# Cached attention decode: longer rows a load, another order of keys, scores after PV

## The chip, the cores and the metric

The kernel runs on one core of one Trainium2 chip. The metric is the time of one execution on the device in microseconds; lower is better. Runs of the kernel before took 1207.76 to 1209.6 us, with a median of 1208.69.

## What is computed

One decode step of a network with two kinds of layers, twice over the same weights and caches: attention over a long cache, then a small SiLU block.

```python
B, Sq, D = 8, 1, 512
Hq, Hkv, Sk, Dh = 32, 8, 8192, 128

def _A_ref(x, k_cache, v_cache, wq, wo):
    q = (x @ wq).reshape(B, Sq, Hq, Dh)              # to (B, Hq, Sq, Dh)
    k = jnp.repeat(k_cache, rep, axis=1)             # rep = 4 query heads a cache head
    v = jnp.repeat(v_cache, rep, axis=1)
    scores = jnp.einsum("bhqd,bhkd->bhqk", q, k) * (Dh ** -0.5)
    p = _softmax(scores, axis=-1)
    o = jnp.einsum("bhqk,bhkd->bhqd", p, v)
    return o.reshape(B, Sq, Hq * Dh) @ wo

def _B_ref(x, w1, w2):                               # F = 1792
    return _silu(x @ w1) @ w2

x = x + _A_ref(_layernorm(x), K, V, wq, wo)
x = x + _B_ref(_layernorm(x), w1, w2)
x = x + _A_ref(_layernorm(x), K, V, wq, wo)
x = x + _B_ref(_layernorm(x), w1, w2)
```

All arrays are bf16. Each of the two caches has 8 batches x 8 heads x 8192 keys x 128 numbers, 134 MB, and both attention layers read both of them.

## The kernel before

**Tasks.** A task is one (layer, batch, cache head). There are 128 of them, and `make_tasks` (L141) lays them out in one list in which the two layers are mixed: while layer 0 works on batch b + 1, layer 1 works on batch b. A task has 8 steps ("positions"; `GPT = 8`), a step covers 8 chunks of 128 keys, and two steps make a granule of 2048 keys, which is the unit of a load: 512 KB, 128 partitions with 4096 bytes each. A head has 4 granules of K and 4 of V.

**Kept heads.** The last 18 granules of K of a batch (half of head 3, heads 4 to 7) stay in SBUF in their transposed form from layer 0 until layer 1 has used them; the layer-1 tasks of these heads ("kept tasks") load only V and transpose nothing. All other tasks are "streaming tasks". For each batch the list has a run of five layer-1 tasks with kept K, then the five layer-0 tasks that fill these heads for the next batch, then five or six streaming tasks.

**Slots and the planner.** SBUF has an arena of 27 slots of one granule. `plan_loads` (L172) lists all 880 loads. Each has a step at which it is needed (`need`) and one after which its slot is free again (`free`). The list is sorted by need, each load takes the slot that comes free first, and `after` is the step after which SP may issue it. `issue` (L352) sends it from SP's queue; SP waits there until the last readers of the slot are done, and everything behind it waits too.

**The main loop** (L748) goes over the steps p and emits, in this order, for all engines:

- `emit_t_until(p + LT)` with `LT = 2`: K of step p + 2 is transposed on TensorE (L433, 8 transposes into one of 3 PSUM banks) and copied back into its own slot by VectorE (L441) or ScalarE (L439, 3 of 8);
- at odd p, first the scores of the granule of steps p - 1 and p (`emit_s`, L464: 4 matmuls of 512 columns), then PV for the two steps 13 and 12 back (`emit_pv`, L537: 2 x 8 matmuls);
- a part of the softmax of the task before: row maximum (L475) and `spread` (L477) at phase 0; a matmul with `ones` that hands every partition the maxima (L485), then `own`, `shift` and the exponential (L488 to L495) at phase 1; the sums (L501, L504) at phase 3; the transposes of P and the copy into `PT` (L513, L517) at phase 4, one step before the first PV that reads it;
- one piece of the "chain", where one is in progress: once layer 0's attention of batch b is complete, the rest of that batch's way to layer 1's query (wo, layer norm at L559 to L602, w1, SiLU, w2, layer norm, wq; matmuls at L613 and L631) is done in small pieces, one or two a step, and has to be through before the first layer-1 task of that batch;
- the normalisation of a finished task (L551) and `issue_until(p)`, which emits the loads whose `after` has come.

Each load has a semaphore of its slot, so the engines wait for a slot's own load. TensorE, VectorE, ScalarE and SP each work in program order. At the end come the sums of heads for layer 1, the last SiLU block for all batches, and the store.

Of the kernel before, what the change touches and what calls it, by code (L numbers as in the profile page):

```python
# [5 lines left out]
HQ = 32  # L6
# [7 lines left out]
GPT = 8  # L14
GPG = 2
NSLOT = 27
KEEP = 18
LT = 2
PRE = 10
LP = 12  # L20
# [4 lines left out]
NPT = 2  # L25
NQB = 2
NST = 4
# [102 lines left out]
class Load:  # L130


    __slots__ = ("kind", "b", "g", "k", "need", "free", "slot", "after")

    def __init__(self, kind, b, g, k, need, free):
        self.kind, self.b, self.g, self.k = kind, b, g, k
        self.need, self.free = need, free
        self.slot, self.after = None, None
# [32 lines left out]

def plan_loads(tasks, kept, nslot, ngran):  # L172

    at = {t: i for i, t in enumerate(tasks)}
    loads = []
    for i, (layer, b, g) in enumerate(tasks):
        for k in range(ngran):
            i0 = i * GPT + k * GPG
            if layer == 0 or (g, k) not in kept:
                need = -1 if i0 < PRE else i0 - LT  # L180
                last = i if layer or (g, k) not in kept else at[(1, b, g)]
                loads.append(Load("K", b, g, k, need, last * GPT + (k + 1) * GPG - 1))
            loads.append(Load("V", b, g, k, i0 + GPG - 1 + LP, i0 + GPG - 1 + LP))
    loads.sort(key=lambda d: (d.need, d.kind))
    free = [(-2, s) for s in range(nslot)]
    for d in loads:
        free.sort()
        d.after, d.slot = free.pop(0)
        assert d.after < d.need or d.need == -1 and d.after == -2, (d.kind, d.need, d.after)
        free.append((d.free, d.slot))  # L190
    return loads
# [18 lines left out]
def _build(ctx, nc, A_x, A_k_cache, A_v_cache, A_wq, A_wo, B_w1, B_w2, out):  # L210
# [59 lines left out]
    QB = [sb([128, NGRAN - 1 + QUAD], BF16, "QB") for _ in range(NQB)]  # L270
    at1 = [sb([128, HQ], BF16, "at1") for _ in range(3)]
    at2 = sb([128, HQ, B], BF16, "at2")
    vr = sb([128, B], FP32, "vr")
    yr = sb([128, B], FP32, "yr")
    tr = sb([128, B], FP32, "tr")
    s1 = sb([128, B], FP32, "s1")
    s1a = sb([128, B], FP32, "s1a")
    xc = sb([128, KT, B], FP32, "xc")
    sq = sb([128, KT, B], FP32, "sq")
    xnT = sb([128, KT, B], BF16, "xnT")  # L280
    eh = sb([128, FT * B], FP32, "eh")
    hsT = sb([128, FT * B], BF16, "hsT")
# [3 lines left out]
    PT = [sb([128, CPB, NQ * USED], BF16, "PT") for _ in range(NPT)]  # L286
    ones = sb([128, 128], FP32, "ones")
    hm = sb([128, REP], FP32, "hm")
    real = sb([128, 1], FP32, "real")
    far = sb([128, NQ * USED], FP32, "far")  # L290
    rowmax = sb([128, 1], FP32, "rowmax")
    spread = sb([128, NQ * USED], FP32, "spread")
    own = sb([128, NQ * USED], FP32, "own")
    shift = sb([128, 1], FP32, "shift")
    rs = [sb([128, 1], FP32, "rs") for _ in range(NST)]
    ssm = [sb([128, REP], FP32, "ssm") for _ in range(NST)]
    ssa = [sb([128, REP], FP32, "ssa") for _ in range(NST)]
    rcp = [sb([128, REP], FP32, "rcp") for _ in range(NST)]

# [52 lines left out]
    def issue(d):  # L352
        cache = A_k_cache if d.kind == "K" else A_v_cache
        src = cache[d.b, d.g].rearrange("(k p c) d -> k p (c d)", k=NGRAN, p=128)[d.k]
        dst = ARENA[:, d.slot * SLOT:(d.slot + 1) * SLOT]
        dma(sp, dst, src, slsem[d.slot], writes=[r_half(d.slot, 0), r_half(d.slot, 1)])
        (k_slot if d.kind == "K" else v_slot)[(d.b, d.g, d.k)] = d.slot

    with nc.Block() as block:

        @block.sync
        def _(sync_eng):
# [11 lines left out]
            op(dve, lambda: dve.memset(ones[:, :], 1.0), writes=["ones"])  # L374
            for n in range(NQB):
                op(pool, lambda n=n: pool.memset(QB[n][:, :], 0.0), writes=[f"QB{n}"])
# [4 lines left out]
                    hm[:, :], lanes.rearrange("p c (r k) -> p r c k", k=NGRAN), AX.XY, ALU.add),  # L381
                reads=["ident"], writes=["hm"],
            )
            op(dve, lambda: dve.tensor_reduce(real[:, :], hm[:, :], AX.X, ALU.add), reads=["hm"], writes=["real"])
            for c in range(NQ):
                op(dve, lambda c=c: dve.tensor_scalar(
                    far[:, c * USED:(c + 1) * USED].rearrange("p (r k) -> p r k", k=NGRAN),
                    hm[:, :].unsqueeze(2).to_broadcast([128, REP, NGRAN]), real[:, 0:1], -FAR,
                    op0=ALU.subtract, op1=ALU.mult),
                   reads=["hm", "real"], writes=["far"])  # L390
# [15 lines left out]
            for _n in range(NGRAN):  # L406
                issue(queue.pop(0))
# [65 lines left out]
            def softmax_max(ti):  # L473
                bank = ti % NSCP
                op(dve, lambda: dve.tensor_reduce(rowmax[:, :], SCp[bank][:, :], AX.X, ALU.max),  # L475
                   reads=[f"SC{bank}"], writes=["rowmax"])
                op(dve, lambda: dve.tensor_scalar(  # L477
                    spread[:, :].rearrange("p (c q) -> p c q", q=USED), lanes, rowmax[:, 0:1], -SM_SCALE,
                    op0=ALU.mult, op1=ALU.mult),
                   reads=["ident", "rowmax"], writes=["spread"])  # L480

            def softmax_shift(ti):
                ob = ti % 2
                every = OTp[ob][:, 0:NQ * USED]
                mm_group([lambda: pe.matmul(every, ones[:, :], spread[:, :], start=True, stop=True)],  # L485
                         reads=["ones", "spread"], writes=[f"OT{ob}"])

                op(dve, lambda: dve.scalar_tensor_tensor(  # L488
                    own[:, :], every, real[:, 0:1], far[:, :], op0=ALU.mult, op1=ALU.add),
                   reads=[f"OT{ob}", "real", "far"], writes=["own"])  # L490
                op(dve, lambda: dve.tensor_reduce(shift[:, :], own[:, :], AX.X, ALU.min), reads=["own"], writes=["shift"])  # L491

            def softmax_exp(ti):
                bank, st = ti % NSCP, ti % NST
                op(act, lambda: act.activation(  # L495
                    P[:, :], SCp[bank][:, :], ACT.Exp, bias=shift[:, 0:1], scale=SM_SCALE, accum_out=rs[st][:, :]),
                   reads=[f"SC{bank}", "shift"], writes=["P", f"rs{st}"])

            def softmax_sum(ti):
                st = ti % NST  # L500
                op(dve, lambda: dve.tensor_scalar(  # L501
                    ssm[st][:, :], hm[:, :], rs[st][:, 0:1], None, op0=ALU.mult),
                   reads=["hm", f"rs{st}"], writes=[f"ssm{st}"])
                op(pool, lambda: pool.partition_all_reduce(ssa[st][:, :], ssm[st][:, :], 128, bass.bass_isa.ReduceOp.add),  # L504
                   reads=[f"ssm{st}"], writes=[f"ssa{st}"])

            def emit_pt(ti):
                pb = ti % NPT
# [9 lines left out]
                    PT[pb][:, :, :].rearrange("p x (c q) -> p x c q", q=USED),  # L518
                    tpv.rearrange("p x (c q) -> p x c q", q=QUAD)[:, :, :, 0:USED]),
                   reads=[f"TP{tb}"], writes=[f"PT{pb}"])  # L520

            def softmax_rcp(ti):
                st = ti % NST
                op(dve, lambda: dve.reciprocal(rcp[st][:, :], ssa[st][:, :]), reads=[f"ssa{st}"], writes=[f"rcp{st}"])

            def emit_pv(i):
# [3 lines left out]
                ob, pb = ti % 2, ti % NPT  # L530
                pv = PT[pb][:, :, :].rearrange("p x (c r k) -> p x c k r", c=NQ, k=NGRAN)
# [10 lines left out]
                mm_group(steps, reads=[r_half(slot, h), f"PT{pb}"], writes=[f"OT{ob}"])  # L542

            def emit_norm(ti):
# [6 lines left out]
                op(dve, lambda: dve.tensor_tensor(dst, OTp[ob][:, 0:REP * PVN:PVN], rcp[st][:, :], ALU.mult),  # L551
                   reads=[f"OT{ob}", f"rcp{st}"], writes=[rd])

            def ln_stages(xv, rx, n):

                xcv, sqv, xnv = xc[:, :, 0:n], sq[:, :, 0:n], xnT[:, :, 0:n]
# [7 lines left out]
                def second():  # L564
# [6 lines left out]
                        reads=["s1a", rx], writes=["xc"],  # L571
                    )
                    op(dve, lambda: dve.tensor_tensor(sqv, xcv, xcv, ALU.mult), reads=["xc"], writes=["sq"])
                    op(dve, lambda: dve.tensor_reduce(s1[:, 0:n], sqv.rearrange("p k b -> p b k"), AX.X, ALU.add),
                       reads=["sq"], writes=["s1"])
                    op(pool, lambda: pool.partition_all_reduce(s1a[:, 0:n], s1[:, 0:n], 128, bass.bass_isa.ReduceOp.add),
                       reads=["s1"], writes=["s1a"])
                def third():
                    v, y = vr[:, 0:n], yr[:, 0:n]
                    vi, yi = v.bitcast(INT32), y.bitcast(INT32)  # L580
                    op(dve, lambda: dve.tensor_scalar(v, s1a[:, 0:n], 1.0 / D, LN_EPS, op0=ALU.mult, op1=ALU.add),
                       reads=["s1a"], writes=["vr"])
                    op(dve, lambda: dve.tensor_scalar(yi, vi, 1, None, op0=ALU.logical_shift_right),
                       reads=["vr"], writes=["yr"])
# [4 lines left out]
                def newton(rounds):  # L589
                    v, y, t = vr[:, 0:n], yr[:, 0:n], tr[:, 0:n]  # L590
                    for _n in range(rounds):
                        op(dve, lambda: dve.tensor_tensor(t, y, y, ALU.mult), reads=["yr"], writes=["tr"])
                        op(dve, lambda: dve.scalar_tensor_tensor(t, t, -0.5, v, op0=ALU.mult, op1=ALU.mult),  # L593
                           reads=["tr", "vr"], writes=["tr"])
# [3 lines left out]
                def fourth():  # L598
# [3 lines left out]
                       reads=["xc", "yr"], writes=["xnT"])  # L602
# [51 lines left out]
            def block_stages(xs, rxs, n, fine=False):  # L654
# [4 lines left out]

                def expo():  # L660
                    op(act, lambda: act.activation(eh[:, 0:FT * n], MISC[:, 0:FT * n], ACT.Exp, scale=-1.0),
                       reads=["MISC"], writes=["eh"])

                def silu():
                    ev = eh[:, 0:FT * n]
                    op(dve, lambda: dve.tensor_scalar(ev, ev, 1.0, None, op0=ALU.add), reads=["eh"], writes=["eh"])
                    op(dve, lambda: dve.reciprocal(ev, ev), reads=["eh"], writes=["eh"])
                    op(dve, lambda: dve.tensor_tensor(hsT[:, 0:FT * n], MISC[:, 0:FT * n], ev, ALU.mult),
# [169 lines left out]
```

## Time and profile before

| | |
|---|---|
| runs, median | 1208.69 us |
| the profiled execution, span | 1205.7 us |
| mean granted TensorE clock | 0.977 |
| HBM read | 473.44 MB, 393 GB/s over the span |
| loads of K and V | 368 and 512, of 512 KB each |
| K load, issue to landing (median) | 15.1 us |
| V load, issue to landing (median) | 10.7 us |
| PE waiting for K (L433), in total | 92.0 us |
| SP waiting for the scores (L464) to free a slot, in total | 229.7 us |
| K copy on VectorE / on ScalarE, one | 690 ns / 1010 ns |
| PT copy L517, row maximum L475, `spread` L477, one | 285, 684, 254 ns |
| exponential L495, one | 687 ns |

A line of the windows view gives a stretch in us, its length, the busy time of each engine with its number of instructions, then the granted TensorE clock, the share of the DMA engines' time that packets took, and GB/s. A line of the timeline gives start and duration in us, the engine, the line and the operation, and in square brackets the idle time before it with what ended it. A packet is one contiguous piece that one DMA engine moves; here one row of one partition.

### The profile page before, as it was taken

The page shows a single profiled execution, that of the slowest core. Times are in us where ns is not written, and L with a number is a line of the kernel's source. Part 1 is how long each engine was busy: PE and PEld are TensorE (multiplying, and loading weights), DVE is VectorE, ACT ScalarE, POOL GpSimd, SP SyncE. Part 2 cuts the span into 40 slices and gives each one's busy share as a digit, 9 for nine tenths or more (in the row PEclk, how much of TensorE's full clock was granted, in tenths as well). Part 3 has the DMA queues.
Part 4 walks back from the last instruction along what each step waited for, and adds up shares of the span by engine and source line. Part 5 has one row for each costly group of instructions (what it writes and reads, how often), then busy time and mean ns, then how long its engine had stood idle before and what let it go on. Part 6 is the DMA issues. An engine that isn't in the chain of part 4 may idle for free.

```text
span 1205.7 us, 45853 instructions
## 1 busy us (share of the span) xinstructions
PE 981.2 (81%) x20216; PEld 772.2 (64%) x20216; DVE 611.8 (51%) x1853; ACT 386.1 (32%) x670; POOL 70.8 (6%) x172
## 2 busy tenths in 40 slices
PE   2868898778888788878888898788888898889885
PEld 2656675667666676667666676667666675667564
DVE  2534564446445554546454554446454554456443
ACT  1323332333233332333233332333233333333231
POOL 0000000000000000000000000000000000000000
PEclk7889999999999999999999999999999999999996
DMA  9999999999999999999999999999999999999994
GB/s 370 385 398 408 403 405 406 408 406 399 396 408 408 408 371 404 408 407 403 399 408 407 405 378 408 409 407 395 385 408 407 401 402 407 408 404 398 390 408 172
DMA packets 133926, 476.43 MB, mean 395 GB/s; under 512 B 14160, under 2 KB 20064, under 8 KB 133216
## 3 DMA queue, kind: packets, MB, share of 16 engines
q1 hardware_dynamic: 133728, 473.51, 99.6%
q8 instruction: 159, 2.61, 0.9%
q14 instruction: 39, 0.32, 0.1%
HBM read 473.44 MB, written 0.01 MB: 393 GB/s over the span
## 4 chain that ended last, share of the span: by engine, by line
DMA 47%; PE 32%; DVE 11%; issue 5%; SPq 3%; ACT 2%; POOL 0%; POOLq 0%; ACTq 0%; DVEq 0%
DMA arena<-in_A_k_cache_dram 45%; PE TPp L433 9%; PE OTp L537 9%; PE SCp L464 5%; PE MISC L613 5%; DVE arena L441 3%; SPq L334 3%; DMA arena<-in_A_v_cache_dram 2%; ACT P L495 2%; PE OTp L485 2%; PE TPp L513 1%; DVE rowmax L475 1%; DVE PT L517 1%; PE MISC L631 1%; DVE tr L593 1%
## 5 line engine op out<-in xcount | busy, mean ns | idle before, releaser
L441 DVE COPY arena<-TPp 128x1024 bf16<-128x1024 bf16 x460 | 317.1, 690 | 384.0 <-PE TPp L433 383.6
L433 PE MATMUL TPp<-ident,arena 128*128 128x128 bf16 x5888 | 418.5, 221 | 110.4 <-DMA arena<-in_A_k_cache_dram 92.0
L433 PEld LDWEIGHTS TPp<-ident,arena 128*128 128x128 bf16 x5888 | 341.3, 99 | 129.7 <-DMA arena<-in_A_k_cache_dram 108.9
L439 ACT COPY arena<-TPp 128x1024 bf16<-128x1024 bf16 x276 | 278.7, 1010 | 395.5 <-PE TPp L433 395.4
L537 PEld LDWEIGHTS OTp<-PT,arena 128*128 128x128 bf16 x8192 | 243.1, 96 | 158.7 <-issue 104.5
L537 PE MATMUL OTp<-PT,arena 128*128 128x48 bf16 x8192 | 296.0, 184 | 33.3 <-DVE at L551 9.6
L464 PE MATMUL SCp<-arena,QB 128*32 128x512 bf16 x2048 | 206.8, 394 | 4.9 <-issue 2.1
L495 ACT ACTIVATE P<-SCp,shift 128x512 bf16<-128x512 f32 x128 | 88.0, 687 | 381.7 <-DVE shift L491 261.9
L504 POOL PARTITION_ALL_REDUCE ssa<-ssm x128 | 56.2, 439 | 940.8 <-DVE ssm L501 923.4
L475 DVE TENSOR_REDUCE rowmax<-SCp 128x1 f32<-128x512 f32 x128 | 87.5, 684 | 33.8 <-PE SCp L464 33.8
L464 PEld LDWEIGHTS SCp<-arena,QB 128*32 128x32 bf16 x2048 | 52.9, 93 | 53.0 <-issue 3.3
L485 PE MATMUL OTp<-spread,ones 128*128 128x64 f32 x256 | 55.2, 297 | 28.4 <-DVE spread L477 27.1
L513 PE MATMUL TPp<-ident,P 128*128 128x128 bf16 x512 | 50.0, 220 | 21.9 <-ACT P L495 20.2
L488 DVE SCALAR_TENSOR_TENSOR own<-OTp,real,far 128x64 f32<-128x64 f32 x128 | 36.3, 284 | 53.4 <-PE OTp L485 53.2
L485 PEld LDWEIGHTS OTp<-spread,ones 128*128 128x128 f32 x256 | 38.6, 190 | 36.9 <-DVE spread L477 35.5
L501 DVE TENSOR_SCALAR ssm<-hm,rs 128x4 f32<-128x4 f32 x128 | 28.8, 225 | 42.8 <-ACT P L495 42.8
L513 PEld LDWEIGHTS TPp<-ident,P 128*128 128x128 bf16 x512 | 32.0, 98 | 26.8 <-ACT P L495 23.8
L613 PE MATMUL MISC<-xnT,wq 128*128 128x32 bf16 (+1 forms) x1152 | 38.7, 176 | 4.2 <-issue 2.8
L517 DVE COPY PT<-TPp 128x256 bf16<-128x256 bf16 x128 | 36.4, 285 | 9.6 <-PE TPp L513 9.6
L631 PE MATMUL MISC<-at,wo 128*128 128x32 bf16 (+1 forms) x1152 | 39.9, 175 | 0.3 <-DVE at L551 0.3
L613 PEld LDWEIGHTS MISC<-xnT,wq 128*128 128x128 bf16 x1152 | 35.0, 96 | 5.3 <-issue 3.2
L631 PEld LDWEIGHTS MISC<-at,wo 128*128 128x128 bf16 x1152 | 35.3, 97 | 0.4 <-DVE at L551 0.4
(47 smaller groups left out, 296.3 us busy)
## 6 DMA issues: line engine op xcount, KB each, us to landing
arena<-in_A_v_cache_dram SPq DMA_DIRECT2D x512, 512.0 KB, 10.7
arena<-in_A_k_cache_dram SPq DMA_DIRECT2D x368, 512.0 KB, 15.1
wq<-in_A_wq_dram SPq DMA_DIRECT2D x1, 4096.0 KB, 16.3
wo<-in_A_wo_dram SPq DMA_DIRECT2D x1, 4096.0 KB, 26.5
w<-in_B_w_dram SPq DMA_DIRECT2D x2, 1792.0 KB, 23.1
P<-in_A_x_dram SPq DMA_DIRECT2D x1, 8.0 KB
out_dram<-P SPq DMA_DIRECT2D x1, 8.0 KB
```

What stands on the lines that cost most here:

```text
L433: lambda c=c: pe.transpose(tpv[:, c, :], chunk(slot, h * GRP + c), ident[:, :])
L439: op(act, lambda: act.copy(dst, TPp[tb][:, :]), reads=[f"TP{tb}"], writes=[r_half(slot, h)])
L441: op(dve, lambda: dve.tensor_copy(dst, TPp[tb][:, :]), reads=[f"TP{tb}"], writes=[r_half(slot, h)])
L464: lambda c=c: pe.matmul(SCp[bank][c * QUAD:(c + 1) * QUAD, :], QB[qn][:, NGRAN - 1 - k:NGRAN - 1 - k + QUAD], ARENA[:, slot * SLOT + c * K ...
L475: op(dve, lambda: dve.tensor_reduce(rowmax[:, :], SCp[bank][:, :], AX.X, ALU.max), reads=[f"SC{bank}"], writes=["rowmax"])
L485: mm_group([lambda: pe.matmul(every, ones[:, :], spread[:, :], start=True, stop=True)], reads=["ones", "spread"], writes=[f"OT{ob}"])
L495: op(act, lambda: act.activation(P[:, :], SCp[bank][:, :], ACT.Exp, bias=shift[:, 0:1], scale=SM_SCALE, accum_out=rs[st][:, :]), reads=[f" ...
L504: op(pool, lambda: pool.partition_all_reduce(ssa[st][:, :], ssm[st][:, :], 128, bass.bass_isa.ReduceOp.add), reads=[f"ssm{st}"], writes=[f ...
L513: lambda c=c: pe.transpose(tpv[:, c, :], P[:, c * 128:(c + 1) * 128], ident[:, :])
L537: lambda c=c, cc=cc: pe.matmul(otp, chunk(slot, h * GRP + c), pv[:, cc % CPB, cc // CPB % NQ, k, :].unsqueeze(2).to_broadcast([128, REP, P ...
L613: lambda o=o, k=k: pe.matmul(MISC[:, o * n:o * n + w], w_sb[:, k, o * 128:(o + 1) * 128], rhs_of(k).to_broadcast([128, w]) if n == 1 else ...
L631: lambda o=o, h=h: pe.matmul(MISC[:, o * w:(o + 1) * w], wo_sb[:, h, o * 128:(o + 1) * 128], rhs_of(h).to_broadcast([128, w]) if n == 1 el ...
```

## The change

- **Keys.** Partition p now holds the 64 consecutive keys 64p to 64p + 63 of a head, and granule k is keys 16k to 16k + 15 of each partition. Before, a granule was 2048 consecutive keys, 16 on each partition. Softmax and PV take K and V in the same order, so what is computed stays the same. Several granules of one head are now contiguous in a partition's row, so one DMA can load 2 or 4 of them with rows of 8192 or 16384 bytes; the rows of two partitions lie 16 KB apart in memory.
- **Loads.** Streamed K and V are loaded in pairs of granules into two neighbouring slots. A kept head has fixed slots ("home") and is loaded in one DMA of 4 granules (head 3: 2). The planner takes loads from a heap by need, picks slots by how early they come free, may use an empty home for streaming if it is given back in time, and splits a pair in two where no place leaves 7 us by its own clock.
- **Order.** `LT` goes from 2 to 1, and at odd p PV comes ahead of the scores.
- **28 slots** in place of 27. The room comes from small buffers: one `PT` in place of two, `spread` and `own` inside `P`, two sets of softmax sums in place of four, scratch of the layer norm and the SiLU in `P`, `PT` and one shared tensor, `ones` as one column read 128 times, `far` as one row of 16 read 4 times.

```diff
-NSLOT = 27
+NSLOT = 28
-LT = 2
+LT = 1
+KWIDE = 2
+VWIDE = 2
+EARLIEST = {1: 0.0, 2: 7.0, 4: 14.0}
+ENOUGH = 14.0
+AHEAD = 10.0
+PACE = (1.24, 0.64)
-NPT = 2
-NST = 4
+NST = 2
...
+def make_homes(kept, nslot, ngran):
+    homes, slot = {}, nslot - len(kept)
+    for g in sorted({g for g, _k in kept}):
+        ks = tuple(k for k in range(ngran) if (g, k) in kept)
+        homes[g] = (ks, slot)
+        slot += len(ks)
+    return homes
...
+    def push(kind, i, ks, home=None):
+        layer, b, g = tasks[i]
+        i0 = i * GPT + ks[0] * GPG
+        if kind == "K":
+            need = -1 if i0 < PRE else i0 - LT
+            end = i if home is None else at[(1, b, g)]
+            free = [end * GPT + (k + 1) * GPG - 1 for k in ks]
+        else:
+            need = i0 + GPG - 1 + LP
+            free = [i * GPT + (k + 1) * GPG - 1 + LP for k in ks]
+        heapq.heappush(heap, (need, kind, i, ks, Load(kind, i, b, g, ks, need, free, home)))
...
+    while heap:
+        d = heapq.heappop(heap)[-1]
+        n = len(d.ks)
+        if d.home is not None:
+            for m in range(n):
+                reserved[d.home + m].pop(0)
+        else:
+            best = None
+            for slot in range(nslot - n + 1):
+                held = free[slot:slot + n]
+                if any(r and lead(r[0], f) < AHEAD for r, f in zip(reserved[slot:slot + n], d.free)):
+                    continue
+                after = max(held)
+                waste = sum(clock[max(0, after)] - clock[max(0, f)] for f in held)
+                key = (-min(lead(d.need, after), ENOUGH), waste, -after, slot)
+                best = key if best is None else min(best, key)
+            if n > 1 and (best is None or -best[0] < EARLIEST[n]):
+                push(d.kind, d.task, d.ks[:n // 2])
+                push(d.kind, d.task, d.ks[n // 2:])
+                continue
+            d.slot = best[-1]
+        d.after = max(free[d.slot:d.slot + n])
+        free[d.slot:d.slot + n] = d.free
+        loads.append(d)
...
     def issue(d):
         cache = A_k_cache if d.kind == "K" else A_v_cache
-        src = cache[d.b, d.g].rearrange("(k p c) d -> k p (c d)", k=NGRAN, p=128)[d.k]
-        dst = ARENA[:, d.slot * SLOT:(d.slot + 1) * SLOT]
+        n = len(d.ks)
+        rows = cache[d.b, d.g].rearrange("(p c) d -> p (c d)", p=128)
+        src = rows[:, d.ks[0] * SLOT:(d.ks[0] + n) * SLOT]
+        dst = ARENA[:, d.slot * SLOT:(d.slot + n) * SLOT]
...
-                mm_group([lambda: pe.matmul(every, ones[:, :], spread[:, :], start=True, stop=True)],
-                         reads=["ones", "spread"], writes=[f"OT{ob}"])
+                mm_group([lambda: pe.matmul(every, ones.to_broadcast([128, 128]), spread, start=True, stop=True)],
+                         reads=["ones", "P"], writes=[f"OT{ob}"])
...
                 emit_t_until(p + LT)
                 if p % GPG == GPG - 1:
-                    if p < NG:
-                        emit_s(p)
                     for i in range(p - LP - GPG + 1, p - LP + 1):
                         if 0 <= i < NG:
                             emit_pv(i)
+                    if p < NG:
+                        emit_s(p)
```

## Prediction

> **What bounds the kernel now.** I read the page's summary first (engines, DMA shares, queues), then its chain of waits, then the windows view at several stretches, and last the timeline of TensorE in one bad stretch.
>
> ```profile
> span 1205.7 us, 45853 instructions
> PE 981.2 (81%) x20216; PEld 772.2 (64%) x20216; DVE 611.8 (51%) x1853; ACT 386.1 (32%) x670; POOL 70.8 (6%) x172
> ...
> q1 hardware_dynamic: 133728, 473.51, 99.6%
> ...
> DMA 47%; PE 32%; DVE 11%; issue 5%; SPq 3%; ACT 2%; POOL 0%; POOLq 0%; ACTq 0%; DVEq 0%
> ```
>
> The queue that SP feeds keeps the sixteen DMA engines occupied for 99.6% of the span, and no compute engine comes near that. The chain of waits agrees: almost half of it is DMA, above all K arriving (45%). The 32% of PE in it tells that some stretches hang on TensorE all the same. The windows show which:
>
> ```profile
> 10.00:16.00 6.00, 2.73 (x26) 2.46 (x24) 1.34 (x7) 1.01 (x1) 0.00 (x0) 1.00 1.01 422
> 88.00:128.00 40.00, 32.50 (x634) 25.77 (x630) 19.86 (x51) 14.51 (x23) 1.73 (x4) 1.00 1.03 408
> 420.00:440.00 20.00, 16.74 (x421) 14.48 (x422) 12.87 (x47) 5.68 (x10) 1.21 (x3) 1.00 0.98 374
> 440.00:460.00 20.00, 17.51 (x385) 13.44 (x383) 8.38 (x27) 5.64 (x12) 1.32 (x3) 0.91 1.00 380
> 840.00:860.00 20.00, 17.16 (x404) 13.67 (x401) 9.03 (x29) 6.02 (x13) 1.32 (x3) 1.00 1.00 370
> ```
>
> The last number is GB/s, the one before it the DMA share. The quiet streams (88 to 128 us, likewise 200 to 260 and 480 to 540) run flat at 408. The dips (374, 380, 370) come once a batch, where the layer-1 chain of that batch (layer norm, w1, w2, wq at L613) is threaded between the attention steps. Taking (408 - rate)/408 x 20 us over all the 20-us windows below 401 between 140 and 1140 us gives 14 us of lost DMA time, 1.75 us a batch. The first row is the one the change turns on: from 10 to 16 us only wq is in flight, 128 partitions by rows of 8192 B, and it runs at 422.
>
> ```profile
> 421.18 0.56 PE L537 MATMUL OTp<-PT,arena 128*128 128x48 bf16 x16 [1.31 <-DVE at L551]
> 421.58 0.85 PE L613 MATMUL MISC<-xnT,w 128*128 128x32 bf16 x28
> 422.29 0.61 PE L433 MATMUL TPp<-ident,arena 128*128 128x128 bf16 x8
> 422.73 0.86 PE L613 MATMUL MISC<-xnT,w 128*128 128x32 bf16 x28
> ```
>
> In such a dip TensorE itself is late: PV waited 1.31 us for VectorE, which has the layer norm's small operations ahead of it, and then w1 stands between the transposes.
>
> **Part 1, longer rows.** Writing out both lists of loads gives 880 loads of 512 KB before; after it 256 V and 120 K loads of 1 MB and 32 K loads of 2 MB (no pair is split), 408 in all, with the same 461.4 MB. A row of a partition grows from 4096 to 8192 or 16384 B. Two prices. By the windows: 461.4 MB at 408 is 1130.8 us, at 422 it is 1093.3: -37.5. By the trace's single packet records: a 4096 B packet has a median of 160 ns, an 8192 B packet of wq 309 ns, the packet of a load's semaphore 9.5 ns (one an engine and load). Before: 112640 x 160 / 16 + 880 x 9.5 = 1134.8 us. After: 48128 x 309 / 16 + 4096 x 607 / 16 + 408 x 9.5 = 1088.8 (607 is an estimate, 309 plus the same step again): -46.0. I take the middle, **-41.8 us**. SP's own work shrinks as well (880 issues of 0.33 to 1.03 us in the timeline become 408) and hides behind the full queue both times.
>
> **Part 2, how far the loads run ahead.** From the same lists I add up, at each step p, the DMA time of what SP may have issued and what is not yet needed. In the streaming tasks, where the chain runs, it was 7.7 to 9.0 us, mean 8.35. After, a cycle of four steps has 9.9, 7.4, 7.4 and 5.0, mean 7.4: at every fourth step a V pair and a K pair come free together, and just then only two pairs are on the way. This includes the 28th slot and the K need that comes one step later. In the kept stretches it falls from as much as 30 us to some 10 to 15, which costs nothing: their least value stays at 7.4.
>
> What is that worth? Setting the start of each score group (L464) against the running sum of 1.289 us for each 512 KB needed by then, TensorE is 2.9, 4.1, 6.1, 3.5, 4.9, 4.9, 3.1 and 3.9 us late at the ends of the eight chains, mean 4.2, of which 1.75 became DMA idle time; the lead swallowed the other 2.5. After, three things add to the idle time of a batch. The DMAs are 3.3% quicker over some 45 us in which TensorE sets the pace and gains nothing: **+1.5**. The lead is shorter: 0.95 by the means, 2.7 by the worst step; a late TensorE meets all four steps, so I take **+0.95**. New waits on TensorE (part 3): **+0.2**. Together 2.65 x 8 = **+21.2 us**, with ends of 1.5 x 8 = 12 and (1.5 + 2.7 + 0.9) x 8 = 41.
>
> **Part 3, the order on TensorE.** Scores go behind PV, and K is transposed one step ahead of the step in hand instead of two. No matmul is added or dropped (16 transposes 1.07 us, scores 0.40, PV 0.57 a granule in the timeline). PV now follows a softmax's transposes (L513) with one transpose group between, not also the scores: its cover for the PT copy (0.285 us, behind a 0.69 us K copy on DVE) loses 0.34 us, the scores' pace in that timeline. The max of a row loses 0.42 us of PV as cover. Behind the waiting PV stand the scores and the next transposes, and SP, which waits for their slots. Bounds: 0 to 0.75 us a task. In the streams TensorE is idle some 0.65 us a granule waiting for K, so it hides. In the chain a projection piece of 0.40 us lies in between; I take 0.06 us a task there, 3.5 tasks, 0.2 us a batch. In kept tasks (no transposes to cover) the whole 0.75 may show, but DMA has slots to refill meanwhile.
>
> **Part 4, the rest at nothing.** One PT, two softmax sets, `spread` and `own` inside P, shared scratch for the layer norm: each new writer comes in program order behind the last reader (PV of the task before ends a step ahead of the next PT transposes). TensorE's order covers them; without it one PT copy of 0.285 us a task would show. `ones` as a repeated column and `far` as a repeated row keep the shapes of L485 and L488; if the weight load (190 ns, twice a task) doubled, 0.38 us a task would go into the same idle 0.65 us. At the start the first K pair lands 1.29 us later than a single, covered by wq, which lands later still. At the end two V granules instead of one follow the last landing: **+0.6** (one PV group of 0.57).
>
> **Sum.** 1205.7 - 41.8 + 21.2 + 0.6 = 1185.7 for the span. The median of the runs is 1208.69, 3.0 above the span, so **1189 us**.
>
> **The rivals.**
> (A) As summed. By its bounds, -46 with +12 and -37.5 with +41: 1175 to 1213; its own likely range 1179 to 1201.
> (B) The lead is enough, and idle time hardly grows. For it: PE waited for K 92 us in all, so it has room. Against it: eight dips already at 7.7 us. -41.8 to -46 with +5 to +10: 1168 to 1178, at 1173.
> (C) Slower or level: one mechanism, the double release at every fourth step. When a K pair has landed, the two pairs on the way last 5.0 us; TensorE needs a transpose group, PV and scores (some 1.3 us), SP 0.3 to 0.8 us for two issues, and an issued load took at least 4.1 us to land on a drained queue, 2.8 without its own transfer. That is 4.4 to 4.9 of 5.0: it decides as soon as TensorE is 0.1 to 0.6 us late. If it does so all along the streams, half a microsecond in each of 12 cycles a batch, that is 48 us on top of the worst +41: 1205.7 - 41.8 + 41 + 48 = 1253, with half of the cycles 1229, with the chain alone 1205; 3.0 more each in the runs. I put it at 1222. Against it: outside the chain TensorE waits for K, so it is not late.
> (D) The change does not give the rate: rows that lie 16 KB apart in memory instead of next to each other cost as much as two 4096 B packets (320 ns). wq's rows lie next to each other, so the 422 says nothing of it. Then only 472 semaphore packets of 9.5 ns are saved, -4.5, and about +15 stays of the idle time: 1219. The Trainium skill (DMA: Bandwidth & Descriptors, Latency and other measured facts) states that a power-of-two row pitch lowers the rate, 207 of 214 GB/s at a 512 KiB pitch; no run here has such a pitch, and 16 KB is far below that one.
>
> **Chances.** A 0.47, B 0.25, C 0.20, D 0.08. About 0.2% (2.4 us) is what a measurement of this kernel can tell from no change. B whole and nearly all of A are faster: 0.71; level, from the edges of A and C: 0.09; slower, most of C and D: 0.20. The range leaves out the low end of B and the part of C and D above 1217: 1167 to 1217.
>
> **What would show it.** Right: packets 8192 B, 408 loads, quiet windows at 420 to 425 GB/s, dips still once a batch and about 4 us each. Wrong in part 1: quiet windows near 408 with TensorE waiting for K. Wrong in part 2 towards B: dips as shallow as before; towards C: DMA share under 1.0 in the quiet windows too, with SP waiting for PE. Wrong in part 3: a wait of PE L537 on the PT copy in most tasks of a chain. The forecast fails as a whole if the quiet windows don't get quicker.

## The result and the profile after

| | before | after |
|---|---|---|
| runs, median | 1208.22 us (1207.33 to 1209.6) | 1244.26 us (1243.08 to 1251.99) |
| ratio, with its 95% interval | | 1.0314 [1.0295, 1.0334] |
| profiled execution, span | 1205.7 us | 1243.0 us |
| mean granted TensorE clock | 0.977 | 0.953 |
| K and V loads | 880 | 408 |

The changed kernel is 36 us slower; the forecast was 20 us faster. First the page of the kernel after: the summary, the rate in 40 equal slices of the span, and the loads with the median time from issue to landing.

```profile
span 1243.0 us, 44907 instructions
PE 998.4 (80%) x20216; PEld 801.1 (64%) x20216; DVE 617.1 (50%) x1850; ACT 386.3 (31%) x670; POOL 70.5 (6%) x172
...
GB/s 383 378 423 403 381 355 422 423 360 365 397 420 418 371 340 422 422 360 370 391 423 402 372 351 422 419 354 333 395 421 406 359 390 424 415 345 362 402 419 111
...
q1 hardware_dynamic: 65760, 473.47, 95.6%
...
arena<-in_A_v_cache_dram SPq DMA_DIRECT2D x256, 1024.0 KB, 9.4
arena<-in_A_k_cache_dram SPq DMA_DIRECT2D x120, 1024.0 KB, 9.4
arena<-in_A_k_cache_dram SPq DMA_DIRECT2D x32, 2048.0 KB, 14.2
```

Both halves of the story stand in the GB/s line. Its peaks are 422 to 424, where the quiet streams of before ran at 408: the longer rows give the rate that was hoped for. Between the peaks lie one or two slices in a row of 333 to 372; before, the lowest slices were single ones of 371 to 390. The queue is occupied for 95.6% of a longer span, 1188 us, against 99.6% of the shorter one, 1201 us.

The windows view of the kernel after shows where the DMAs idle (columns as before: the last three numbers are the granted clock, the DMA share, GB/s).

```profile
260.00:280.00 20.00, 15.90 (x304) 12.56 (x301) 10.28 (x26) 7.20 (x12) 0.82 (x2) 0.96 0.93 339
280.00:300.00 20.00, 16.82 (x374) 14.57 (x372) 12.05 (x43) 6.10 (x10) 1.31 (x4) 0.95 0.97 368
500.00:520.00 20.00, 16.71 (x340) 13.97 (x338) 11.05 (x27) 7.61 (x12) 0.86 (x2) 1.00 1.01 422
860.00:880.00 20.00, 15.66 (x344) 13.37 (x344) 8.93 (x23) 5.62 (x11) 0.88 (x2) 0.91 0.80 305
```

The chain's projection matmuls (L693) of that batch run from 294 to 318 us. The window 260 to 280 lies ahead of them, in a plain stream, and is the worse one at 339. The kernel before in the same windows:

```profile
260.00:280.00 20.00, 16.65 (x332) 13.40 (x328) 10.13 (x28) 7.47 (x12) 0.86 (x2) 1.00 1.02 401
280.00:300.00 20.00, 17.67 (x390) 14.14 (x388) 13.97 (x59) 7.78 (x13) 2.46 (x6) 1.00 1.02 400
```

Summed in slices of 1 us from 80 us to the landing of the last load, bytes missing against 408 GB/s before and 422 after come to:

| lost DMA time, us | before | after |
|---|---|---|
| in the eight chains (from 12 us ahead of the first chain matmul) | 9.0 | 46.9 |
| in the 33 us ahead of each of these | 0.8 | 28.6 |
| everywhere else | 7.9 | 11.9 |
| sum | 17.7 | 87.4 |

How it happens is seen in the queue's own timeline of the kernel after (start, duration, engine, line), around the start of the chain at 294 us:

```profile
285.07 0.33 SPq L412 DMA_DIRECT2D arena<-in_A_v_cache_dram  x1
285.51 0.37 SPq L412 DMA_DIRECT2D arena<-in_A_k_cache_dram  x1
290.48 0.33 SPq L412 DMA_DIRECT2D arena<-in_A_v_cache_dram  x1
291.19 0.33 SPq L412 DMA_DIRECT2D arena<-in_A_k_cache_dram  x1
297.00 0.33 SPq L412 DMA_DIRECT2D arena<-in_A_v_cache_dram  x1
297.43 0.37 SPq L412 DMA_DIRECT2D arena<-in_A_k_cache_dram  x1
```

and in the DMA view of 284 to 300 us (busy tenths and GB/s in slices of 0.4 us):

```profile
DMA  9999799957999999999999599999999993396899
GB/s 471 348 410 451 328 369 225 348 225 287 451 430 410 389 430 430 389 430 410 410 389 307 246 430 430 410 410 430 389 410 471 410 410 123 82 287 164 287 389 410
```

A V pair and a K pair go out together, and from the start of the second issue nothing more for 5.0 to 5.8 us. Two pairs are 4.96 us of transfer at 423 GB/s. Ahead of the chain the rate already sinks to 225 twice (286.4 to 287.6); at 297.2, within its first pieces, the engines have run dry (123 and 82 GB/s) while the next two pairs have only just been issued. Over the whole execution, the waits of SP (releaser, us in total, times, longest) say who holds the issue back; after:

```profile
SPq L96 <- PE OTp L616: 723.7, 178, 11.8
```

and before:

```profile
SPq L90 <- PE SCp L464: 229.7, 146, 3.5
SPq L90 <- PE OTp L537: 176.5, 128, 3.1
```

Before, SP was held about 275 times for some 1.5 us each. After, it is held 178 times for 4.1 us each, by PV, which frees the slots for the load that stands first in SP's program order (in the lines above a V pair); the other pair waits behind it. This wait by itself is no measure of a loss: in e11 below, the fastest kernel, the same line reads 751.8 us in 267 waits.

On TensorE new waits appear. The waits of the kernel after:

```profile
PE TPp L512 <- DMA arena<-in_A_k_cache_dram: 37.9, 31, 8.2
PE OTp L616 <- DVE at L630: 29.9, 69, 1.3
PE SCp L543 <- ACT arena L518: 29.9, 27, 1.2
PE SCp L543 <- DVE arena L520: 22.9, 57, 1.1
```

and before:

```profile
PE TPp L433 <- DMA arena<-in_A_k_cache_dram: 92.0, 148, 9.0
PE OTp L537 <- DVE at L551: 9.6, 9, 1.3
PE SCp L464 <- DVE arena L441: 0.5, 3, 0.2
```

So after the change TensorE waits less for K (37.9 us in place of 92.0), and the last three rows come to 83 us, where the kernel before had 10. The second line needs a word: PV does not read `at`. The normalisation L630 is the short VectorE operation right behind the copy into `PT` (L596), which PV does read (in a stream of e1, below, it ends 0.08 us after that copy); I read this line as the wait for `PT`.

### The profile page after: what moved, and what is told of

It is laid out like the page before. It is cut to its first block, busy times and chain, and to the rows that moved or that the text cites. A ratio compares the mean times of both kernels' runs of the same rounds, so it can differ in the third digit from the quotient of the medians.

```text
span 1243.0 us, 44907 instructions
## 1 busy us (share of the span) xinstructions
PE 998.4 (80%) x20216; PEld 801.1 (64%) x20216; DVE 617.1 (50%) x1850; ACT 386.3 (31%) x670; POOL 70.5 (6%) x172
## 3 DMA queue, kind: packets, MB, share of 16 engines
q1 hardware_dynamic: 65760, 473.47, 95.6%
## 5 line engine op out<-in xcount | busy, mean ns | idle before, releaser
L512 PE MATMUL TPp<-ident,arena 128*128 128x128 bf16 x5888 | 434.6, 224 | 57.3 <-DMA arena<-in_A_k_cache_dram 37.9
L616 PEld LDWEIGHTS OTp<-PT,arena 128*128 128x128 bf16 x8192 | 265.2, 98 | 99.6 <-issue 74.4
L576 ACT ACTIVATE P<-SCp,small 128x512 bf16<-128x512 f32 x128 | 87.9, 687 | 416.2 <-DVE small L572 224.6
L554 DVE TENSOR_REDUCE small<-SCp 128x1 f32<-128x512 f32 x128 | 87.9, 687 | 80.2 <-PE SCp L543 80.0
L584 POOL PARTITION_ALL_REDUCE small<-small x128 | 56.0, 437 | 969.6 <-DVE small L582 951.3
L596 DVE COPY PT<-TPp 128x256 bf16<-128x256 bf16 x128 | 36.8, 287 | 77.9 <-PE TPp L592 77.9
L567 DVE SCALAR_TENSOR_TENSOR P<-OTp,small 128x64 f32<-128x64 f32 x128 | 36.3, 284 | 72.2 <-PE OTp L564 72.0
L564 PEld LDWEIGHTS OTp<-P,small 128*128 128x128 f32 x256 | 39.2, 192 | 50.6 <-DVE P L556 36.7
L564 PE MATMUL OTp<-P,small 128*128 128x64 f32 x256 | 57.1, 306 | 15.9 <-DVE P L556 15.4
L582 DVE TENSOR_SCALAR small<-small 128x4 f32<-128x4 f32 x128 | 28.9, 226 | 42.0 <-ACT P L576 42.0
L693 PEld LDWEIGHTS MISC<-small,wq 128*128 128x128 bf16 x1024 | 31.8, 97 | 6.9 <-issue 6.2
L693 PE MATMUL MISC<-small,wq 128*128 128x32 bf16 x1024 | 35.4, 178 | 0.9 <-issue 0.9
```

The source lines that it names most:

```text
L512: lambda c=c: pe.transpose(tpv[:, c, :], chunk(slot, h * GRP + c), ident[:, :])
L554: op(dve, lambda: dve.tensor_reduce(rowmax, SCp[bank][:, :], AX.X, ALU.max), reads=[f"SC{bank}"], writes=["rowmax"])
L564: mm_group([lambda: pe.matmul(every, ones.to_broadcast([128, 128]), spread, start=True, stop=True)], reads=["ones", "P"], writes=[f"OT{ob}"])
L576: op(act, lambda: act.activation(P[:, :], SCp[bank][:, :], ACT.Exp, bias=shift, scale=SM_SCALE, accum_out=rs[st]), reads=[f"SC{bank}", "sh ...
L584: op(pool, lambda: pool.partition_all_reduce(ssa[st], ssm[st], 128, bass.bass_isa.ReduceOp.add), reads=[f"ssm{st}"], writes=[f"ssa{st}"])
L616: lambda c=c, cc=cc: pe.matmul(otp, chunk(slot, h * GRP + c), pv[:, cc % CPB, cc // CPB % NQ, k, :].unsqueeze(2).to_broadcast([128, REP, P ...
```

## The experiments

Two theories could explain the loss. **L, the lead of the loads:** pairs that come free together leave too little on the way. **O, the order on TensorE:** with PV ahead of the scores and K transposed one step ahead, TensorE waits for copies that used to be covered, and frees slots late. "Old order" below means LT = 2 with scores ahead of PV. The kernel before took 1207.1, 1208.1 and 1207.0 us beside the runs e1 to e4, e5 to e8 and e9 to e11. All kernels compute the whole result.

**e1: the change with streamed loads of one granule** (kept heads still in one DMA).

```diff
-KWIDE = 2
-VWIDE = 2
+KWIDE = 1
+VWIDE = 1
```

> The changed kernel with all streamed loads single again (512 KB), everything else as changed: rows of 4096 B, still 16 KB apart; order on TensorE, 28 slots, homes stay. Theory L (lead): pairs leave only 5.0 us of DMA work on the way at every fourth step, so the DMAs idle; single loads have 9.0 to 11.6 us, so the quiet windows run at 408 GB/s and the dips are no deeper than before: 1190 to 1208 us. Theory O (order): TensorE is late because PV comes ahead of the scores and K is transposed one step ahead; that stays, so 1225 us or more. Theory D (pitch): rows 16 KB apart cost rate; quiet windows under 400 GB/s.

Measured 1231.77 us (1229.58 to 1233.23), 1.0203 [1.0187, 1.0218]. Without pairs, with at least 9.0 us of lead everywhere, the kernel is still 25 us slower than before. L alone cannot be the answer. The waits of TensorE in e1:

```profile
PE SCp L543 <- ACT arena L518: 34.2, 31, 1.5
PE OTp L616 <- DVE at L630: 32.0, 70, 1.6
PE SCp L543 <- DVE arena L520: 25.7, 65, 1.1
...
PE TPp L512 <- DMA arena<-in_A_k_cache_dram: 9.3, 4, 5.3
```

The loads are practically always there in time (9.3 us), and the scores wait 59.9 us for K's copies. The timeline of TensorE in a stream of e1 shows both waits in their place:

```profile
361.17 1.07 PE L512 MATMUL TPp<-ident,arena 128*128 128x128 bf16 x16
362.08 0.56 PE L616 MATMUL OTp<-PT,arena 128*128 128x48 bf16 x16
362.99 0.40 PE L543 MATMUL SCp<-arena,QB 128*32 128x512 bf16 x4 [0.35 <-DVE arena L520]
...
367.01 0.56 PE L616 MATMUL OTp<-PT,arena 128*128 128x48 bf16 x16 [0.29 <-DVE at L630]
```

Transposes, PV, scores of the same granule: PV's 0.56 us is shorter than what the last copy of K (0.69 us on VectorE, 1.01 on ScalarE) takes from its transposes on.

**e2: the change with scores ahead of PV again, K still one step ahead.**

```diff
+                    if p < NG:
+                        emit_s(p)
                     for i in range(p - LP - GPG + 1, p - LP + 1):
                         if 0 <= i < NG:
                             emit_pv(i)
-                    if p < NG:
-                        emit_s(p)
```

> The changed kernel with the scores ahead of PV again, K still transposed one step ahead. L: lead unchanged, 1232 to 1255 us. O by PV ahead of the scores: at least 20 us faster than the changed kernel, 1224 or less. The scores now have one transpose group less between them and the copy of K that they read, so a wait of the scores on that copy of up to 0.4 us a granule is possible; then slower than 1255.

Measured 1279.2 us, 1.0598 [1.0573, 1.0623], the slowest of all. Its waits:

```profile
PE SCp L543 <- DVE arena L520: 88.4, 164, 1.0
PE SCp L543 <- ACT arena L518: 59.9, 71, 1.6
```

With K one step ahead, PV is what stands between K's transposes and its scores. Take it away and the scores wait 148 us for copies. The two halves of the new order belong together; half of it tells nothing of the whole, and this run does not separate L from O.

**e3: the change in the old order** (pairs kept).

```diff
-LT = 1
+LT = 2
...
+                    if p < NG:
+                        emit_s(p)
                     for i in range(p - LP - GPG + 1, p - LP + 1):
                         if 0 <= i < NG:
                             emit_pv(i)
-                    if p < NG:
-                        emit_s(p)
```

> The changed kernel with the whole order of before on TensorE (scores ahead of PV, K transposed two steps ahead), still pairs; the planner's lead is 9.9, 7.5, 5.0, 5.0 in a cycle of four steps, so it has the short lead at two steps in place of one. L: 1235 to 1270 us. O: 1215 or less.

Measured 1245.7 us (1237.64 to 1246.69), 1.0305 [1.0272, 1.0337]: no better than with the new order. O alone cannot be the answer either. Here the waits of TensorE are of the other kind:

```profile
PE TPp L512 <- DMA arena<-in_A_k_cache_dram: 104.8, 86, 8.6
```

and the windows of e3 show the same idle DMAs as after, in the stream ahead of the chain:

```profile
260.00:280.00 20.00, 18.12 (x354) 14.44 (x352) 12.46 (x31) 8.73 (x14) 0.86 (x2) 1.00 0.88 326
500.00:520.00 20.00, 18.14 (x316) 14.56 (x316) 10.41 (x26) 7.61 (x12) 0.86 (x2) 0.85 1.01 422
```

Lost DMA time, counted as in the table above: 55.7 in the chains, 27.0 ahead of them, 10.5 elsewhere, 93.2 in all. The planner of this run split six K pairs (12 loads of 512 KB); all other streamed loads are pairs.

**e4: the kernel before with the new order** (singles, 27 slots, old layout).

```diff
-LT = 2
+LT = 1
...
-                    if p < NG:
-                        emit_s(p)
                     for i in range(p - LP - GPG + 1, p - LP + 1):
                         if 0 <= i < NG:
                             emit_pv(i)
+                    if p < NG:
+                        emit_s(p)
```

> The kernel before with the new order alone (PV ahead of the scores, K one step ahead), single loads of before, 27 slots. L: lead 7.7 and 10.3 us, no shorter than before: 1200 to 1214 us. O: 1225 or more.

Measured 1226.09 us (1221.71 to 1237.56), 1.0172 [1.012, 1.0224]. The order alone costs the kernel before 19 us, though its lead by the list of loads is 10.3 and 7.7 us, no less than before (9.0 and 7.7). In its profiled execution, the quickest of the four (1221.7 us), the lost DMA time is 28.4 us against 17.7 before: 15.8 in the chains (before 9.0), 1.6 ahead of them (0.8) and 11.0 elsewhere (7.9). From the last landing to the end of the span it took 18.1 us in place of 15.1. So for the kernel before, most of what the order adds in lost DMA time comes in the chains, and 3 us at the end. L and O are both there, and either is enough for a loss. Four more runs took them apart.

**e5: the change with neither** (single loads, old order: e1's and e3's edits together). What is left of the change is the layout of the keys, the homes of kept heads, the planner, 28 slots and the shared buffers.

> The changed kernel without its two suspects: single streamed loads and the order of before; 28 slots, the shared small buffers, the key layout and the kept heads in one load stay. Theory of two causes (L: pairs shorten the lead; O: the new order makes TensorE late): neither is left, the lead is 9.0 to 10.3 us and the DMA work 1122.6 us instead of 1131.0, so 1190 to 1206 us. If the shared buffers or the rows 16 KB apart cost something of their own: 1215 or more.

Measured 1203.3 us (1201.88 to 1207.28), 0.9966 [0.9955, 0.9977]. The rest of the change, taken together, gains some 5 us; e5 doesn't tell its parts apart. With the lists' DMA times (estimates: 1.285 us a granule in a single by 408 GB/s, 1.242 in a pair by 422 GB/s, 1.226 in a load of four by its packets of 613 ns) a table of two by two results, medians in us:

| | single streamed loads | pairs |
|---|---|---|
| old order | 1203.3 (e5) | 1245.7 (e3) |
| new order | 1231.8 (e1) | 1244.3 (after) |
| DMA time of the list | 1122.6 | 1091 |

Pairs cost 42 us in the old order and 12 in the new one. The new order costs 28 us with singles and nothing with pairs. The costs do not add up. I read this so: each makes TensorE or the loads late, and where one of them already is the bound, the other hides behind it.

**e6: the kernel before with two slots less**, which takes its lead to 6.4 and 5.1 us and leaves everything else.

```diff
-NSLOT = 27
+NSLOT = 25
```

> The kernel before with 25 slots in place of 27 and nothing else: single loads, old order, lead 5.1 and 6.4 us. L in its plain form (the time that loads run ahead decides, whatever their size): 1222 us or more. If it is the size of the pairs instead (a pair lands late as a whole): 1216 or less.

Measured 1226.64 us (1224.09 to 1229.72), 1.0144 [1.0125, 1.0163]. Lead by itself has its price, 18.5 us for 2.6 us less; the lost DMA time goes from 17.7 to 39.7 us. But e3, whose least lead is the same 5.0 and whose mean lead is larger (6.9 against 5.75), is at 154 us above the DMA time of its list; e6 is at 96, the kernel before at 77. So a lead of 5 us that consists of two loads may be worse than one of four. This is not shown: e3 and e6 differ in more than the size of the loads, and where TensorE sets the pace a list with less DMA time gains nothing, which alone makes the distance to it larger.

**e7: the kernel before with PV ahead of the scores, K still two steps ahead** (only the second hunk of e4).

> The kernel before with PV ahead of the scores, K still transposed two steps ahead. If the cost of the new order lies in K one step ahead (the scores wait for the copies of K): 1202 to 1214 us. If it lies in PV ahead of the scores (PV waits for the copy of PT, K and V slots come free together): 1220 or more.

Measured 1216.11 us (1212.59 to 1217.25), 1.0059 [1.0042, 1.0077]: between what was expected for the one and for the other, so both halves of the order cost. PV first costs 8 us; K one step ahead the other 11 or so of e4. The wait of e7:

```profile
PE OTp L537 <- DVE at L551: 47.7, 92, 1.6
```

There are 92 waits of half a microsecond for `PT` in 128 tasks (before: 9 waits, 9.6 us in all).

**e8: pairs only where the lead allows, old order.** The planner splits a pair where no place leaves 10 us by its own clock, and lends out a home only if 14 us are left.

```diff
-LT = 1
-EARLIEST = {1: 0.0, 2: 7.0, 4: 14.0}
-AHEAD = 10.0
+LT = 2
+EARLIEST = {1: 0.0, 2: 10.0, 4: 14.0}
+AHEAD = 14.0
```

(and scores ahead of PV, as in e3)

> The changed kernel with the order of before, and pairs only where the planner finds a lead of 10 us or more by its clock (and homes lent for streaming given back 14 us early): 36 K and 138 V pairs are left, 404 singles, lead 7.5 to 10.3 us in the streams, DMA work 1108 us. Two causes: both are gone and a part of the quicker rows stays, 1178 to 1198 us. If pairs cost by their size and not by the lead: 1205 or more.

Measured 1193.12 us (1190.76 to 1196.27), 0.9876 [0.9857, 0.9894]: faster than both kernels. The list now has 174 pairs, 404 singles and the 32 loads of four, a least lead of 7.5 us, and 1108 us of DMA time.

**e9: as e3, but with 16 kept granules instead of 18**: all pairs, old order, two more slots for the streams. Lead 12.4, 9.9, 7.5, 7.5; 8.4 MB more to load (DMA time 1111 against 1092).

```diff
-KEEP = 18
+KEEP = 16
```

> Pairs everywhere and the order of before, but 16 kept granules a batch in place of 18: two slots more for streaming (a lead of 12.4, 9.9, 7.5, 7.5 us in a cycle of four steps where the pairs with 18 have 9.9, 7.5, 5.0, 5.0), for 8.4 MB more to load (DMA work 1111 us, against 1091.6). L: the lead counts and not the size of a pair, so 1185 to 1210 us although it loads more. If pairs cost by their size: 1240 or more.

Measured 1205.61 us (1203.94 to 1209.95), 0.9994 [0.998, 1.0007]. It has 19 us more to load and is 40 us faster than e3; the lost DMA time falls from 93.2 to 33.5 us. So a pair as such does not cost 42 us. What hurts most is pairs with only two of them on the way. One reserve: with 16 kept granules the list of tasks changes as well (runs of four kept heads a batch in place of five, and more streaming tasks), and 16 kept granules with 26 slots, which would bring the short lead back into this list, was not run. Against e5's singles the distance to the list's DMA time is still 14 us larger (94.6 and 80.7); whether the size of the pairs costs that is open.

**e10: as e9 in the new order.**

> The same with the new order of the changed kernel (PV ahead of the scores, K one step ahead), lead 12.4, 9.9, 9.9, 7.5 us. O as a cause of its own: with the lead given, TensorE is the bound again, 12 to 30 us slower than the same with the order of before, TensorE waiting little for K. If the order only cost through the lead: the same time within 8 us.

Measured 1219.24 us (1217.49 to 1219.71), 1.0094 [1.0078, 1.0111]. Once the lead is there the order costs 13.6 us again, which it did not between e3 and after. TensorE still waits 42.0 us for K there (e9: 76.4), more than was expected.

**e11: e8 with a limit of 9.5 us and the old AHEAD of 10.** 200 pairs, least lead 7.5, DMA time 1106.

> As the version with pairs only where the lead is long, with the bound at 9.5 us and homes lent until 10 us before they are needed: 44 K and 156 V pairs, 352 singles, least lead still 7.5 us, DMA work 1106 us. L: within 6 us of the version with 10 us (1193), on the quicker side if anything.

Measured 1191.73 us (1190.97 to 1193.73), 0.9872 [0.9854, 0.9889], the fastest; its ranges overlap those of e8, so the two are not told apart. Its windows, in the same places as above:

```profile
260.00:280.00 20.00, 18.24 (x364) 14.46 (x360) 12.45 (x42) 8.94 (x15) 1.93 (x5) 1.00 1.03 408
280.00:300.00 20.00, 18.28 (x443) 15.36 (x440) 13.10 (x51) 6.39 (x11) 1.38 (x4) 1.00 1.02 407
500.00:520.00 20.00, 18.05 (x371) 14.52 (x368) 11.19 (x28) 8.73 (x14) 0.86 (x2) 1.00 1.01 421
```

421 in the quiet stream as in the changed kernel, 407 to 408 where that had 339 and 368.

## Why the prediction was wrong

**Part 1, the rows (-41.8): right.** Quiet windows at 421 to 424; a packet of 8192 B has a median of 309 ns in this trace too, one of 16384 B 613 ns (the estimate was 607); 408 loads, none split. The DMA time of the lists, by these rates, went from 1131 to 1091 us, 40 less. Rows that lie 16 KB apart cost nothing, so rival D is out. The Trainium skill (DMA: Bandwidth & Descriptors, Rules for kernel authors) gives at least 1 MiB a DMA, over 128 partitions, for maximum bandwidth. For the rate of a full queue this case agrees by 3% (422 against 408 GB/s, with the rows longer as well). The rule speaks of bandwidth alone: e3's 1 MB pairs lose 42 us of the kernel's time against e5's 512 KB.

**Part 2, the lead (+21.2): the step that failed.** The lead of 9.9, 7.4, 7.4 and 5.0 us was counted rightly, and then valued at its mean, 0.95 us a batch, "a late TensorE meets all four steps". The lost DMA time grew by 69.7 us, not 21.2. Two things were wrong in it. First, what happens at the worst step was left out: at the double release two pairs are on the way, they last 5 us, and the loads in the stretch shown took 6.0 to 10.1 us from issue to landing. A step that runs dry delays the next K, and with it PV and the next release, so that the better steps don't make up for it. (That the lateness feeds itself in this way is argued from the timeline; that pairs with a short lead are the cause is shown by e3, e5, e6 and e9. No run tells the least lead from the mean one: in a cycle the least is 5.0 us after, 5.0 in e3 and 5.1 in e6, and 7.5 to 9.0 before and in e5 and e9; the means, 7.4, 6.9 and 5.75 against 8.35 to 9.65, part the same runs. What failed is the price, 0.95 us a batch.) Second, the loss was put into the chains alone, because only they lost time before. 28.6 us of it came in the 33 us ahead of them, where the kernel before lost 0.8.

This is rival C, which had 0.20: one mechanism, double release, with 1253 for all of the streams and 1229 for half of the cycles (3.0 more each in the runs). The 1244.3 measured lies between. What told against it, "outside the chain TensorE waits for K, so it is not late", was, as I read it, the mistake: a TensorE that waits for K releases its slots just as late as one that is busy.

**Part 3, the order (0.06 us a task in chains, hidden in 0.65 us a granule elsewhere): wrong as well, though it adds nothing to this result.** With enough lead it costs 13.6 us (e10 against e9) to 28.5 (e1 against e5). Two waits were priced wrongly. The scores' wait for K's copies was left out: the prediction looked at what PV loses as cover, not at what LT = 1 takes from the scores (59.9 us in e1, 0.5 in the kernel before). And the wait for `PT`, named with bounds of 0 to 0.75 us a task, came 69 times in 128 tasks with 0.43 us each, streams included. The idle 0.65 us a granule does not cover it: counted against 408 GB/s, e1 loses 10 us more DMA time than e5 in the chains, but 9 more ahead of them and 10 more elsewhere. My explanation is that this is idle time of the loads' making, which a TensorE that is late uses up. In e1 the 77.4 us that TensorE waited for K in e5 shrank to 9.3, while the waits for K copies and `PT` grew by 83.

**Part 4, the rest at nothing: not contradicted.** e5 is even 5 us faster than the kernel before, with 8.4 us less DMA time for the kept heads' long rows; a small cost of the shared buffers could hide in that difference. Only the tail was mis-sized: +0.6 was foreseen, and from the last landing to the end of the span it took 20.9 us instead of 15.1, so +5.8 (17.5 in e1, 17.0 in e3, 15.1 in e5: the order and the pairs both lengthen it).

**The sum** by measured terms: 1205.7 - 40 + 69.7 + 5.8 = 1241.2, against a span of 1243.0.

**The rest:** A and B rested on a loss of at most 41 us and did not come. The signs named for C came: a DMA share under 1.0 in a stream ahead of the chain, SP waiting for PE. The sign against part 3, PV waiting for `PT`, came too. The forecast's own condition for failing as a whole, that quiet windows don't get quicker, did not occur: it failed although they did.

## What to carry to other kernels

In a fixed arena a larger DMA needs its bytes twice: once in the buffer that it fills and once in the ones that must be in flight meanwhile. Before loads are widened, write out what is on the way at each step, and hold the step with the least of it, not only the mean, against the measured time from issue to landing; widen only where that allows (e11: 1191.7 us, 0.9872 [0.9854, 0.9889] of the time before, where widening everywhere took 1.0314). And idle time of an engine that waits for loads is no cover to spend on a tighter order: it is gone as soon as the loads come in time, so test a change of order with the loads made early.

## What the runs showed of the hardware

In the kernel before, an issue on SP took 0.33 us (median) with 3 to 7 loads on the way and 1.03 to 1.07 us with 11 or 12. Rows of 8 KB that lie 16 KB apart in memory took 309 ns each, as wq's adjoining ones did, and quiet windows with them ran at 421 to 424 GB/s. The mean granted TensorE clock was 0.977 before and 0.953 after, but it does not follow the time: e6 is 18.5 us slower than the kernel before at 0.977, and e11, the fastest, had 0.960. The record of the clock knows only full and half speed: half speed lasted 58 us in all before, 120 after, 157 in e3, 97 in e11 and 59 in e6. One such spell (from 278.5 us in the kernel after) begins 0.5 us behind 2.2 us in which TensorE waited for K, so it may in part follow from late loads. It does not by itself make the DMAs idle: e3's window of 500 to 520 us has a clock of 0.85 and 422 GB/s. What sets it is open, and so is how much of PE's longer busy time (998.4 against 981.2 us), and of the 36 us, comes from it.
